# Linear attention, routed experts and SoLU block on one Trainium2 core: TensorE's order in the attention stage written out by hand, with the column-tiled matmuls of a step in one series

## The chip, the cores and the metric

The kernel runs on one core of one Trainium2 chip. The metric is the device time of one execution in microseconds (us), from the median of several runs; less is better.

## The reference

Three blocks follow each other. The change touches the first alone. In it q, k and v have 8 batches, 8 heads, 576 tokens and 64 columns; `w_phi` is 64 x 128.

```python
def phi(x):
    proj = np.einsum('bhsd,df->bhsf', x, w_phi)
    proj = proj - np.max(np.abs(proj), axis=-1, keepdims=True)
    return np.concatenate([np.exp(proj), np.exp(-proj)], axis=-1)
q_p, k_p = (phi(q), phi(k))
kv = np.einsum('bhsf,bhsd->bhfd', k_p, v)
z = np.sum(k_p, axis=2)
num = np.einsum('bhsf,bhfd->bhsd', q_p, kv)
den = np.einsum('bhsf,bhf->bhs', q_p, z)[..., None] + 1e-06
return num / den
```

The second block sends each of the 4608 tokens to one of 8 experts, by the argmax of `x @ w_gate + modality_bias`; the third computes a softmax-weighted hidden layer with a normalization over 4608 x 1024 values.

## The kernel before, in words

**Units and steps.** The attention stage works on units of two batches and four heads: 8 units, numbered by `p2` (a pair of batches) and `g` (which four heads, 0 or 1). A unit is 9 steps (72 in all), one for each 128-row group `i` of tokens: `i` from 0 to 3 belong to the first batch ("half 0"), 5 to 8 to the second ("half 1"), and `i` = 4 holds the last 64 tokens of both. A step has one job of k and one of q (in the last unit, the last four steps take two jobs of k or two of q).

**What a step issues on TensorE.** `s0` (line 239) transposes the k and q rows of the coming step, four 128 x 128 transposes at line 248; ScalarE rounds them to `hi` (line 251) and VectorE takes the rest as `lo` (line 252). `proj` (line 255) multiplies by `w_phi` in three parts, six matmuls of 128 x 256 (lines 260 to 262); VectorE finds the largest absolute value (line 264) and subtracts it (line 266); for k, ScalarE takes the two exponentials into `e` (lines 270, 271). Two steps later (`LAGF`), `accum_kv` (line 274, matmul in line 276) adds v times `e` to the tile `kv`, and `q_features` (line 320) transposes the q values (line 323) and takes their exponentials into `qp`. GpSimd sums `e` into `es` (lines 291, 315).

**Whole and tiled array.** The transposes, the projections and the `kf` matmuls (line 352) use all 128 columns of the array. `kv` uses it in two column tiles of 64 (the profile writes 128\*64, and 64\*64 for `i` = 4, whose halves have 64 rows), `num` (line 397) in two tiles of 64, `den` (line 407) and the sum `z` (line 340) in four tiles of 32.

**After a half.** `finish_kv` (line 336) is a Python generator appended to `tasks` when the last `kv` of a half is in: the sum `z`; `kf`, which turns `kv` round; the transpose of `z` (line 367); four `num` parts and two `den` parts; `finish` (line 444), which transposes `den` (line 462) and `num` (line 477) and divides on VectorE (lines 466 to 479); and, for `g` = 1, `gating` (line 486), a chain of small VectorE instructions from line 492 to line 506, two small matmuls that rank the tokens (lines 514, 515: "the ranking matmuls" below), and more VectorE work up to the scatters to DRAM on GpSimd's queue (line 545). There are nine such chains: one for each half of four pairs of batches, the last of which is cut in two.

**What sets the order.** The loop (from line 607) calls `s0` of the coming step first, then the two projections, then `accum_kv` and `q_features` of two steps before, and resumes the generators `RT` = (0, 1, 2, 1, 0) times at five places. This order is only a priority: in this stage the planner places the instructions of TensorE, VectorE, ScalarE and GpSimd by its own estimate of when each is ready. The order that it finds is fixed in the program; on the chip each engine takes its instructions in that order.

**Buffers.** PSUM has three buffers `tp` (transposes, `kf`), four `mm` (projections, `z`, `num`, `den`) and one `kv`.

Of the kernel before, what the change touches and what calls it, by code (L numbers as in the profile page):

```python
# [8 lines left out]
F32 = mybir.dt.float32  # L9
# [8 lines left out]
P = 128  # L18
# [17 lines left out]
YCOLS = PAD + NTOK  # L36
LAG = 8
LAGF = 2
RT = (0, 1, 2, 1, 0)
BGN = 1  # L40
BGP = 100
PRE = 1
# [146 lines left out]
def attention(ctx, tc, c, cnt, xe, q, k, v, ld, early, m, late):  # L189
# [19 lines left out]
    def load_unit(p2, g):  # L209
        u = Unit()  # L210
        u.p2, u.g = p2, g
        u.src = {}
        for half in range(2):
            b = 2 * p2 + half
            for nm in "kqv":
                u.src[nm, half] = ld.tile([P, 4, 4 * D], F32, name="ld" + nm)
            first = p2 == g == half == 0
            w = 4 * D // (2 if first else 1)
            for c0 in range(0, 4 * D, w):
                for nm, t in (("k", k), ("q", q), ("v", v)):  # L220
# [12 lines left out]
        u.qp = [w2p.tile([P, 2, 4, S], F32, name="qp") for _ in range(2)]  # L233
        u.kv = [None, None]
        u.es = [None, None]
        u.qdone = set()
        return u

# [35 lines left out]
    def accum_kv(u, i, e):  # L274
# [39 lines left out]
            for r in range(2):  # L314
                G.tensor_tensor(out=eo, in0=eo, in1=ev[:, :, r, :], op=ALU.add)  # L315
        if i in (4, 8):
            u.kt = w2p.tile([P, 2, 2 * F], F32, name="kt")
            A.copy(u.kt, u.kv[i // 5])

    def q_features(u, i, x):  # L320
        tp = tps.tile([P, 4, P], F32, name="tp")
# [11 lines left out]
                    tp.rearrange("p (h r) t -> p h (r t)", r=2), AF.Exp, scale=sc,  # L333
                )

    def finish_kv(u, half):
        kt = u.kt
        zp = mmp.tile([P, 2 * F], F32, name="mm")
        for h in range(4):
            T.matmul(  # L340
# [5 lines left out]
        yield  # L346
        kf = w2p.tile([P, 2, 4, D], F32, name="kf")
        gdt = gd[(2 * u.g + half) % 2]
        for j in range(2):
            tp = tps.tile([P, 2, P + 2 * E], F32, name="tp")  # L350
            for fh in range(2):
                T.matmul(
                    tp[:, fh, :], lhsT=kt[:, j, fh * F : (fh + 1) * F], rhs=c.idwg[:, 2 * u.g + j, :],
                    start=(fh == 0), stop=True, skip_group_check=True,
                )
            A.copy(
                kf[:, :, 2 * j : 2 * j + 2, :],
                tp[:, :, 0:P].rearrange("p a (h d) -> p a h d", h=2),
            )
            A.copy(  # L360
                gdt[:, :, 2 * j : 2 * j + 2, 0:E],
                tp[:, :, P : P + 2 * E].rearrange("p a (h e) -> p a h e", h=2),
            )
        yield
        tp = tps.tile([P, 2, P], F32, name="tp")
        for fh in range(2):
            T.transpose(tp[:, fh, :], zs[:, fh, :], c.ident)
        A.copy(gdt[:, :, :, E : E + 1], tp.rearrange("p a (h n) -> p a h n", n=32)[:, :, :, 0:1])
        yield
        tiles = (0, 1, 2, 3) if half == 0 else (5, 6, 7, 8)  # L370
# [6 lines left out]
        def keep(dst, pp, c0, c1):  # L377
            off = half * D
            if half == 0 and c1 == S:
                A.copy(dst(2)[:, 0:D], pp[:, c1 - c0 - D :])  # L380
                c1 -= D
            if half == 1 and c0 == 0:
                A.copy(dst(2)[:, D:P], pp[:, 0:D])
                pp, c0 = pp[:, D:], D
            A.copy(dst(half)[:, c0 - off : c1 - off], pp[:, 0 : c1 - c0])

        last = half == 1 and u is last_unit()
        chunks = (((0, 256), (0, 1)), ((256, S), (2, 3, 4)), ((0, 320), (4, 5, 6)), ((320, S), (7, 8)))
        for ci, ((c0, c1), need) in enumerate(chunks[2 * half : 2 * half + 2]):
            while not u.qdone.issuperset(need):  # L390
                yield
            n = c1 - c0
            for j in range(2):
                pp = mmp.tile([P, n], F32, name="mm")
                for fh in range(2):
                    for hh in range(2):
                        T.matmul(
                            pp[hh * D : (hh + 1) * D, :], lhsT=kf[:, fh, 2 * j + hh, :],
                            rhs=u.qp[half][:, fh, 2 * j + hh, c0:c1],
                            start=(fh == 0), stop=(fh == 1), skip_group_check=True,  # L400
                        )
                keep(lambda x: u.num[x][:, j], pp, c0, c1)
                yield
            pp = mmp.tile([P, n], F32, name="mm")
            for fh in range(2):
                for h in range(4):
                    T.matmul(
                        pp[32 * h : 32 * h + 32, :], lhsT=gdt[:, fh, h, :],
                        rhs=u.qp[half][:, fh, h, c0:c1], tile_position=(0, 32 * h),
                        start=(fh == 0), stop=(fh == 1), skip_group_check=True,  # L410
                    )
            keep(lambda x: u.den[x], pp, c0, c1)
            yield
            if last:
                if ci == 0:
                    yield from finish(u, 2, 0, 1)
                else:
                    yield from pend
                yield from finish(u, 1, 2 * ci, 2)
                if ci == 0:  # L420
                    pend = gating(u, 4, 3)
                    next(pend)
                else:
                    pend = gating(u, 7, 2)
                    for n in range(2):
                        for _ in range(FSTEP):
                            next(pend, None)
                        first_slot(n)
                    yield from pend
        if last:  # L430
            return
        yield from finish(u, half, 0, 4)
        if half == 1:
            yield from finish(u, 2, 0, 1)
        if u.g == 1:
            yield
            yield from gating(u, 4 * half, 4 + half)
            if u.p2 == 2 and half == 1:
                early.pick(cnt[0])
                early.ready = True  # L440

    xt, xs, gs = {}, {}, {}

# [116 lines left out]
            U[ui] = load_unit(*units[ui])  # L560
        return U.get(ui)

    tasks = []

    def first_slot(n):
        if n == 0:
            tp = tps.tile([P, 4, P], F32, name="tp")
# [17 lines left out]
    def last_unit():  # L585
        return U.get(len(units) - 1)

    def run_tasks(n):
        for _ in range(n):
            if not tasks:  # L590
                return
            if next(tasks[0], tasks) is tasks:
                tasks.pop(0)

    unit(0)
    zero = w1p.tile([P, ROW], F32, name="zero")
    G.memset(zero, 0.0)
# [6 lines left out]
    n = len(steps)  # L604
    feats = {}
    late()
    for st in range(n + LAGF):
        if st == 9 * 7 + PRE:
            assert early.ready
            m.prefetch()  # L610
        if st == 9 * 7 + STEP0:
            for i in range(RING0):
                m.split_raw(1, i)
        if st + 1 < n:
# [5 lines left out]
        if st < n:  # L620
            h_ = hl.pop(st)
            feats[st] = []
            for a, (kind, i) in enumerate(steps[st][1]):
                feats[st].append((kind, i, proj(h_, a, kind)))
                run_tasks(RT[1 + a])
        if st >= LAGF:
            u = unit(steps[st - LAGF][0])
            for a, (kind, i, x) in enumerate(feats.pop(st - LAGF)):
                if kind == "k":
                    accum_kv(u, i, x)  # L630
                    if i in (4, 8):
                        tasks.append(finish_kv(u, i // 5))
# [800 lines left out]
```

## Time and profile before

| | us |
|---|---|
| median of 3 runs (lowest to highest) | 1386.82 (1385.80 to 1387.13) |
| span of the profiled execution, first to last instruction | 1384.0 |
| attention on TensorE in that span | 7 to 459 |

The profiled execution is told by its span; the runs are times of the device, a little more than a span. The profile is of one execution. A group of rows gives a line of the kernel, engine, operation, output and inputs, and how often; a time on the left of a timeline row is the start in the span, the next the busy time. Matmuls are pipelined: one is shown busy for longer than the distance to the next start, so what the array gives to one is read from start to start. An idle time stands with what ended it.

### The profile page before, as it was taken

How to read it: one execution, taken by the hardware profiler on the slowest of the kernel's cores; microseconds unless marked ns; L12 is line 12 of the kernel's file. 1: busy time of each engine (PE TensorE's matmuls, PEld its weight loads, DVE VectorE, ACT ScalarE, POOL GpSimd, SP SyncE). 2: the span in 40 equal slices, each digit the busy share in tenths (PEclk: the TensorE clock that was granted, in tenths of full speed). 3: DMA queues.
4: the chain of work that ended last, by engine and by line, in shares of the span. 5: the costliest groups of instructions: out<-in, count | busy, mean ns of one | idle time of the engine just before them, and what ended most of it. 6: DMA issues, size and time to landing. Idle time of an engine off the chain costs nothing.

```text
span 1384.0 us, 25538 instructions
## 1 busy us (share of the span) xinstructions
PE 1338.4 (97%) x9522; PEld 1100.7 (80%) x9522; DVE 829.0 (60%) x1524; ACT 660.0 (48%) x1254; POOL 530.5 (38%) x540
## 2 busy tenths in 40 slices
PE   8999999999999989899899999999999999999997
PEld 6666676666666789899899999998989877778885
DVE  7666866767766748889997544443444333334443
ACT  5564665556555425354456444444444333334332
POOL 6555655654664413343323222323323222223331
PEclk9999999999999999999999999999999999999998
DMA  8622232222131223232532111111234154502110
GB/s 230 191 58 91 97 89 85 89 71 79 47 108 62 86 56 93 77 92 62 185 98 70 47 46 54 32 54 46 76 116 157 42 172 156 160 32 61 39 39 23
DMA packets 123120, 120.09 MB, mean 87 GB/s; under 512 B 35664, under 2 KB 109552, under 8 KB 122992
## 3 DMA queue, kind: packets, MB, share of 16 engines
q1 hardware_dynamic: 117008, 99.30, 23.9%
q0 software_dynamic: 5824, 19.04, 3.8%
q8 instruction: 77, 1.26, 0.4%
q14 instruction: 51, 0.42, 0.1%
q10 hardware_dynamic: 160, 0.07, 0.0%
HBM read 148.32 MB, written 33.02 MB: 131 GB/s over the span
## 4 chain that ended last, share of the span: by engine, by line
PE 51%; DVE 7%; issue 4%; ACT 1%; POOL 0%; POOLq 0%; ACTq 0%; DVEq 0%
PE tp L974 32%; PE h L974 15%; PE tp L998 2%; DVE wlo L832 2%; DVE wab L906 2%; PE tp L804 1%; ACT whi L831 1%; PE tp L1249 1%; PE tp L1233 1%; DVE wab L914 0%; DVE w L832 0%; DVE hTl L989 0%; ACT hTh L988 0%; DVE xTl L794 0%; DVE wab L903 0%
## 5 line engine op out<-in xcount | busy, mean ns | idle before, releaser
L315 POOL TENSOR_TENSOR es<-es,e 128x512 f32<-128x512 f32 x128 | 164.1, 1288 | 132.3 <-ACT e L271 120.6
L264 DVE TENSOR_REDUCE m<-mm 128x4 f32<-128x512 f32 x144 | 97.6, 682 | 64.0 <-PE mm L262 62.7
L974 PE MATMUL tp<-hTh,wlo 128*128 128x256 f32 x432 | 123.3, 285 | 8.7 <-DVE wlo L832 8.7
L974 PE MATMUL tp<-hTl,whi 128*128 128x256 f32 x432 | 123.4, 286 | 4.9 <-DVE hTl L989 4.9
L974 PE MATMUL tp<-xTh,whi 128*128 128x256 f32 x432 | 122.5, 283 | 2.2 <-PEq L1312 2.2
L974 PE MATMUL tp<-hTh,whi 128*128 128x256 f32 x432 | 122.6, 284 | 0.0
L974 PE MATMUL tp<-xTh,wlo 128*128 128x256 f32 x432 | 121.6, 282 | 1.0 <-DVE wlo L832 0.7
L974 PE MATMUL tp<-xTl,whi 128*128 128x256 f32 x432 | 121.2, 281 | 0.0
L1133 DVE TENSOR_REDUCE s_mx<-h 128x1 f32<-128x512 f32 x72 | 46.4, 686 | 118.2 <-PE h L974 118.2
L1169 POOL DMA_INDIRECT out_dram<-wab,gt x36 | 38.3, 1063 | 201.9 <-ACT wab L1168 200.8
L1138 ACT ACTIVATE ex<-h,s_mx,gt 128x1024 f32<-128x1024 f32 x36 | 43.4, 1206 | 119.7 <-DVE s_mx L1135 65.9
L260 PE MATMUL mm<-wphi_hi,hi 128*128 128x256 f32 x288 | 90.7, 318 | 3.5 <-ACT hi L251 1.9
L974 PEld LDWEIGHTS tp<-hTh,wlo 128*128 128x128 f32 x432 | 83.3, 193 | 9.8 <-DVE wlo L832 9.5
L974 PEld LDWEIGHTS tp<-hTl,whi 128*128 128x128 f32 x432 | 83.4, 193 | 6.3 <-DVE hTl L989 6.1
L974 PEld LDWEIGHTS tp<-xTh,whi 128*128 128x128 f32 x432 | 82.1, 190 | 2.8 <-ACTq L1312 2.4
L832 POOL TENSOR_TENSOR yTl<-yin,yTh 128x512 fp32r<-128x512 f32 x36 | 46.4, 1290 | 97.7 <-ACT yTh L831 97.6
L974 PEld LDWEIGHTS tp<-hTh,whi 128*128 128x128 f32 x432 | 83.4, 193 | 0.5
L974 PEld LDWEIGHTS tp<-xTh,wlo 128*128 128x128 f32 x432 | 81.9, 190 | 1.4 <-DVE wlo L832 0.9
L262 PE MATMUL mm<-wphi_hi,lo 128*128 128x256 f32 x288 | 82.6, 294 | 0.3 <-DVE lo L252 0.3
L974 PEld LDWEIGHTS tp<-xTl,whi 128*128 128x128 f32 x432 | 82.0, 190 | 0.4
L276 PE MATMUL kv<-e,ldv 128*64 128x256 f32 x512 | 80.6, 394 | 0.9 <-ACT e L271 0.9
L261 PE MATMUL mm<-wphi_lo,hi 128*128 128x256 f32 x288 | 80.5, 282 | 0.0
(427 smaller groups left out, 3951.9 us busy)
## 6 DMA issues: line engine op xcount, KB each, us to landing
ldk<-in_moe_w_dram SPq DMA_DIRECT2D x66, 512.0 KB
ldv<-in_moe_w_dram SPq DMA_DIRECT2D x66, 512.0 KB
ldq<-in_moe_w_dram SPq DMA_DIRECT2D x44, 512.0 KB
yd<-yo SPq DMA_DIRECT2D x36, 256.0 KB
yin<-yd SPq DMA_DIRECT2D x18, 512.0 KB
xin<-xe SPq DMA_DIRECT2D x16, 512.0 KB
ldk<-in_k_dram SPq DMA_DIRECT2D x15, 512.0 KB
ldq<-in_q_dram SPq DMA_DIRECT2D x15, 512.0 KB
```

The lines of the kernel that those rows point to most:

```text
L260: T.matmul(o, lhsT=hi[:, 2 * a + j, :], rhs=c.wphi_hi, start=(j == 0), stop=False, skip_group_check=True)
L261: T.matmul(o, lhsT=hi[:, 2 * a + j, :], rhs=c.wphi_lo, start=False, stop=False, skip_group_check=True)
L262: T.matmul(o, lhsT=lo[:, 2 * a + j, :], rhs=c.wphi_hi, start=False, stop=True, skip_group_check=True)
L264: V.tensor_reduce(out=m, in_=pj, axis=AX.X, op=ALU.max, apply_absolute_value=True)
L276: T.matmul(u.kv[half][(h % 2) * D : (h % 2 + 1) * D, h // 2, :], lhsT=lhsT, rhs=rhs, start=first, stop=last, skip_group_check=True,)
L315: G.tensor_tensor(out=eo, in0=eo, in1=ev[:, :, r, :], op=ALU.add)
L832: eng.tensor_tensor(out=lo, in0=src, in1=hi.bitcast(F32), op=ALU.subtract)
L906: V.tensor_scalar(out=a, in0=b, scalar1=-0x800000, scalar2=None, op0=ALU.bitwise_and)
L974: T.matmul(o, lhsT=l, rhs=r, start=first and n == 0, stop=last and n == 2, skip_group_check=True)
L1133: V.tensor_reduce(out=mx, in_=h[:, sl], axis=AX.X, op=ALU.max, negate=True)
L1138: A.activation(ex, h, AF.Exp, bias=mx, scale=g, accum_out=sm)
L1169: ins = G.indirect_dma_start(out=out, out_offset=bass.IndirectOffsetOnAxis(ap=ys.pop(i)[2].bitcast(I32), axis=0), in_=ob, in_offset=None,)
```

## The change

From here on TensorE takes its instructions in the attention stage in the order in which the program calls them; the other engines are still placed by the planner. The generator of a half becomes a list of items of four kinds: "f" for work on the whole array (`kf`, the transpose of `z`, then `finish` and `gating` as a chain), "64" for a `num` part, "32" for `z` or a `den` part, "0" for the choice of output tiles. A step is now: transposes of q features, projection of k, one "f", projection of q, one "f", `s0` of the coming step, one "f", then `kv`, up to two "64" and up to one "32". The last half runs as a generator of its own, `finish_last`, once all else is done. Function bodies that only move are left out below.

```diff
-RT = (0, 1, 2, 1, 0)
+FSLOT = (1, 1, 1)
+COLS64 = 2
+COLS32 = 1
+TAIL = 1
...
+    ctx.enter_context(tc.manual_schedule(engines={mybir.EngineType.PE}))
...
+    class Item:
+        def __init__(self, kind, fn, after=(), ready=None):
+            self.kind, self.fn, self.after, self.ready, self.done = kind, fn, after, ready, False
+            items.append(self)
+
+        def runnable(self):
+            return all(x.done for x in self.after) and (self.ready is None or self.ready())
...
+    def run_items(kind, count):
+        ran = 0
+        while ran < count:
+            it = next((x for x in items if x.kind == kind and x.runnable()), None)
+            if it is None:
+                break
...
+    def finish_kv(u, half):
+        at = step[0]
+        zi = Item("32", lambda: z_sum(u, half), ready=lambda: step[0] > at)
+        kfs = [Item("f", lambda j=j: kf_part(u, half, j)) for j in range(2)]
+        zt = Item("f", lambda: z_part(u, half), after=[zi])
+        begin = Item("0", lambda: outputs(u, half))
+        parts = []
+        for ci, (_, need) in enumerate(CHUNKS[half]):
+            ok = lambda need=need: u.qdone.issuperset(need)
+            for j in range(2):
+                parts.append(Item("64", lambda ci=ci, j=j: num_part(u, half, ci, j), after=[begin, kfs[j]], ready=ok))
+            parts.append(Item("32", lambda ci=ci: den_part(u, half, ci), after=[begin, zt, *kfs], ready=ok))
+
+        def rest():
+            yield from finish(u, half, 0, 4)
+            if half == 1:
+                yield from finish(u, 2, 0, 1)
+            if u.g == 1:
                 yield
+                yield from gating(u, 4 * half, 4 + half)
+                if u.p2 == 2 and half == 1:
+                    early.pick(cnt[0])
+                    early.ready = True
+
+        Chain("f", rest(), after=parts)
...
     for st in range(n + LAGF):
+        step[0] = st
...
+        run_items("0", 2)
...
+        q_next()
+        if st < n:
+            h_ = hl.pop(st)
+            feats[st] = []
+            for a, (kind, i) in enumerate(steps[st][1]):
+                feats[st].append((kind, i, proj(h_, a, kind)))
+                run_items("f", FSLOT[a])
+                if a == 0:
+                    q_next()
+        else:
+            q_next()
         if st + 1 < n:
             ui, jobs = steps[st + 1]
             if ("k", 5) in jobs:
                 unit(ui + 1)
             hl[st + 1] = s0(unit(ui), jobs)
-        run_tasks(RT[0])
...
+        run_items("f", FSLOT[2])
+        for i, x in kjobs:
+            accum_kv(u_old, i, x)
+            if i in (4, 8):
+                if i == 8 and u_old is last_unit():
+                    tail.append(finish_last(u_old))
                 else:
-                    q_features(u, i, x)
-                    u.qdone.add(i)
-                run_tasks(RT[3 + a])
-    while tasks:
-        run_tasks(1)
+                    finish_kv(u_old, i // 5)
+        run_items("0", 2)
+        run_items("64", COLS64)
+        run_items("32", COLS32)
+        if st >= n and tail:
+            for _ in range(TAIL):
+                next(tail[0], None)
+    while items:
+        for kind in ("0", "f", "64", "32"):
+            run_items(kind, 1)
+        step[0] += 1
+    for _ in tail[0]:
+        pass
```

## Rows read from the trace of the kernel before

**Rows 1.** The page: busy time of the engines, share of the span, instructions
```profile
PE 1338.4 (97%) x9522; PEld 1100.7 (80%) x9522; DVE 829.0 (60%) x1524; ACT 660.0 (48%) x1254; POOL 530.5 (38%) x540
```

**Rows 2.** Windows: stretch and its length, busy us by engine, clock, DMA share, GB/s
```profile
227.16:339.55 112.39, 111.14 (x907) 75.17 (x907) 78.17 (x158) 65.79 (x163) 63.47 (x58) 1.00 0.26 85
```

**Rows 3.** Waits of TensorE, 20 to 440 us: total us, times, longest
```profile
PE mm L260 <- DVE g_sm L522: 1.6, 3, 0.5
PE kv L276 <- ACT e L271: 0.9, 3, 0.3
PE tp L352 <- ACT qp L331: 0.5, 3, 0.2
PE mm L514 <- DVE g_oh L506: 0.5, 3, 0.2
PE mm L262 <- DVE lo L252: 0.3, 1, 0.3
```

**Rows 4.** Timeline of TensorE, 312 to 319 us: kv in pieces, then whole
```profile
312.74 0.65 PE L276 MATMUL kv<-e,ldv 128*64 128x256 f32 x4
313.32 0.66 PE L323 MATMUL tp<-ident,xsq 128*128 128x128 f32 x4
313.91 0.65 PE L276 MATMUL kv<-e,ldv 128*64 128x256 f32 x4
...
317.67 1.08 PE L276 MATMUL kv<-e,ldv 128*64 128x256 f32 x8
318.58 1.03 PE L397 MATMUL mm<-qp,kf 128*64 128x256 f32 x8
```

**Rows 5.** Timeline of TensorE, 303 to 324 us: transposes alone, kv of two forms, den
```profile
303.17 0.60 PE L477 MATMUL tp<-ident,num 128*128 128x128 f32 x4
303.60 0.38 PE L462 MATMUL tp<-ident,den 128*128 128x128 f32 x2
...
305.09 1.08 PE L276 MATMUL kv<-e,ldv 128*64 128x256 f32 x8
306.11 1.08 PE L276 MATMUL kv<-e,ldrv 64*64 64x256 f32 x8
...
322.11 0.28 PE L261 MATMUL mm<-wphi_lo,hi 128*128 128x256 f32 x1
322.22 0.28 PE L262 MATMUL mm<-wphi_hi,lo 128*128 128x256 f32 x1
322.43 1.07 PE L407 MATMUL mm<-qp,gd 128*32 128x256 f32 x16
323.43 0.38 PE L260 MATMUL mm<-wphi_hi,hi 128*128 128x256 f32 x1
323.65 0.28 PE L261 MATMUL mm<-wphi_lo,hi 128*128 128x256 f32 x1
```

**Rows 6.** Timeline of TensorE: first and last of 166 series of column-tiled matmuls
```profile
17.70 1.08 PE L276 MATMUL kv<-e,ldv 128*64 128x256 f32 x8
...
457.01 0.63 PE L407 MATMUL mm<-qp,gd 128*32 128x256 f32 x4
```

**Rows 7.** Timeline of TensorE: den transposes and ranking matmuls, half 0, half 1
```profile
107.96 0.44 PE L462 MATMUL tp<-ident,den 128*128 128x128 f32 x2
...
117.22 0.18 PE L514 MATMUL mm<-g_oh,tri_bf 128*128 128x32 bf16 x1 [0.16 <-DVE g_oh L506]
...
139.97 0.27 PE L462 MATMUL tp<-ident,den 128*128 128x128 f32 x1
...
146.40 0.18 PE L514 MATMUL mm<-g_oh,tri_bf 128*128 128x40 bf16 x1
```

**Rows 8.** Groups of VectorE by form, 227.16 to 339.55 us, the costliest: total and mean ns
```profile
L264 DVE TENSOR_REDUCE m<-mm 128x4 f32<-128x512 f32 x36 | 24.4, 682 | 15.7 <-PE mm L262 15.3
```

**Rows 9.** Windows behind the attention stage, columns as in rows 2
```profile
495.00:500.00 5.00, 1.58 (x13) 1.41 (x12) 0.00 (x0) 0.97 (x2) 0.00 (x0) 0.95 0.38 105
500.00:505.00 5.00, 5.00 (x33) 5.00 (x32) 4.78 (x5) 3.94 (x7) 0.00 (x0) 0.70 0.01 2
```

More of the change, by code (lines that the diff above doesn't have):

```diff
@@ L235, in load_unit @@
         u.es = [None, None]
+        u.kt, u.zs, u.kf = [None, None], [None, None], [None, None]
         u.qdone = set()
@@ L316, in accum_kv @@
         if i in (4, 8):
-            u.kt = w2p.tile([P, 2, 2 * F], F32, name="kt")
-            A.copy(u.kt, u.kv[i // 5])
+            u.kt[i // 5] = w2p.tile([P, 2, 2 * F], F32, name="kt")
+            A.copy(u.kt[i // 5], u.kv[i // 5])
     def q_features(u, i, x):
@@ L334, in q_features, with __init__, z_sum @@
                 )
-    def finish_kv(u, half):
-        kt = u.kt
+    items = []
+    class Item:
[4 more added lines that the diff above has]
+            return all(x.done for x in self.after) and (self.ready is None or self.ready())
+    class Chain(Item):
+        def __init__(self, kind, gen, after=(), ready=None):
+            super().__init__(kind, None, after, ready)
+            self.gen = gen
+    def run_items(kind, count):
[4 more added lines that the diff above has]
+                break
+            if isinstance(it, Chain):
+                if next(it.gen, items) is not items:
+                    ran += 1
+                    continue
+            else:
+                it.fn()
+            it.done = True
+            items.remove(it)
+            ran += 1
+        return ran
+    step = [0]
+    def z_sum(u, half):
         zp = mmp.tile([P, 2 * F], F32, name="mm")
@@ L345, in finish_kv @@
         A.copy(zs, zp.rearrange("p (a f) -> p a f", a=2))
-        yield
-        kf = w2p.tile([P, 2, 4, D], F32, name="kf")
-        gdt = gd[(2 * u.g + half) % 2]
[L349 to L358, printed above, removed]
-            )
[L360 to L363, printed above, removed]
@@ L364, in finish_kv, with kf_part @@
-        yield
+        u.zs[half] = zs
+    def kf_part(u, half, j):
+        if j == 0:
+            u.kf[half] = w2p.tile([P, 2, 4, D], F32, name="kf")
+        kf = u.kf[half]
+        gdt = gd[(2 * u.g + half) % 2]
+        tp = tps.tile([P, 2, P + 2 * E], F32, name="tp")
+        for fh in range(2):
+            T.matmul(
+                tp[:, fh, :], lhsT=u.kt[half][:, j, fh * F : (fh + 1) * F], rhs=c.idwg[:, 2 * u.g + j, :],
+                start=(fh == 0), stop=True, skip_group_check=True,
+            )
+        A.copy(
+            kf[:, :, 2 * j : 2 * j + 2, :],
+            tp[:, :, 0:P].rearrange("p a (h d) -> p a h d", h=2),
+        )
+        A.copy(
+            gdt[:, :, 2 * j : 2 * j + 2, 0:E],
+            tp[:, :, P : P + 2 * E].rearrange("p a (h e) -> p a h e", h=2),
+        )
@@ L365, in finish_kv, with z_part, keep @@
+    def z_part(u, half):
+        gdt = gd[(2 * u.g + half) % 2]
         tp = tps.tile([P, 2, P], F32, name="tp")
         for fh in range(2):
-            T.transpose(tp[:, fh, :], zs[:, fh, :], c.ident)
+            T.transpose(tp[:, fh, :], u.zs[half][:, fh, :], c.ident)
         A.copy(gdt[:, :, :, E : E + 1], tp.rearrange("p a (h n) -> p a h n", n=32)[:, :, :, 0:1])
-        yield
-        tiles = (0, 1, 2, 3) if half == 0 else (5, 6, 7, 8)
+    def keep(half, dst, pp, c0, c1):
+        off = half * D
+        if half == 0 and c1 == S:
+            A.copy(dst(2)[:, 0:D], pp[:, c1 - c0 - D :])
+            c1 -= D
+        if half == 1 and c0 == 0:
+            A.copy(dst(2)[:, D:P], pp[:, 0:D])
+            pp, c0 = pp[:, D:], D
+        A.copy(dst(half)[:, c0 - off : c1 - off], pp[:, 0 : c1 - c0])
@@ new lines, in attention, with num_part @@
+    CHUNKS = (
+        (((0, 256), (0, 1)), ((256, S), (2, 3, 4))),
+        (((0, 320), (4, 5, 6)), ((320, S), (7, 8))),
+    )
+    def num_part(u, half, ci, j):
+        c0, c1 = CHUNKS[half][ci][0]
+        n = c1 - c0
+        pp = mmp.tile([P, n], F32, name="mm")
+        for fh in range(2):
+            for hh in range(2):
+                T.matmul(
+                    pp[hh * D : (hh + 1) * D, :], lhsT=u.kf[half][:, fh, 2 * j + hh, :],
+                    rhs=u.qp[half][:, fh, 2 * j + hh, c0:c1],
+                    start=(fh == 0), stop=(fh == 1), skip_group_check=True,
+                )
+        keep(half, lambda x: u.num[x][:, j], pp, c0, c1)
@@ new lines, in den_part @@
+    def den_part(u, half, ci):
+        c0, c1 = CHUNKS[half][ci][0]
+        n = c1 - c0
+        gdt = gd[(2 * u.g + half) % 2]
+        pp = mmp.tile([P, n], F32, name="mm")
+        for fh in range(2):
+            for h in range(4):
+                T.matmul(
+                    pp[32 * h : 32 * h + 32, :], lhsT=gdt[:, fh, h, :],
+                    rhs=u.qp[half][:, fh, h, c0:c1], tile_position=(0, 32 * h),
+                    start=(fh == 0), stop=(fh == 1), skip_group_check=True,
+                )
+        keep(half, lambda x: u.den[x], pp, c0, c1)
@@ L371, in finish_kv, with outputs @@
+    def outputs(u, half):
         u.num[half] = w1p.tile([P, 2, 4 * P], F32, name=f"num{half}")
@@ L375, in finish_kv @@
             u.den[2] = w1p.tile([P, P], F32, name="den2")
[L377 to L387, printed above, removed]
@@ L388, in finish_kv @@
-        chunks = (((0, 256), (0, 1)), ((256, S), (2, 3, 4)), ((0, 320), (4, 5, 6)), ((320, S), (7, 8)))
-        for ci, ((c0, c1), need) in enumerate(chunks[2 * half : 2 * half + 2]):
-            while not u.qdone.issuperset(need):
-                yield
-            n = c1 - c0
-            for j in range(2):
[L394 to L402, printed above, removed]
-                yield
[L404 to L412, printed above, removed]
-            yield
[L414 to L440, printed above, removed]
+    def finish_kv(u, half):
[15 more added lines that the diff above has]
+            if u.g == 1:
+                yield
+                yield from gating(u, 4 * half, 4 + half)
[3 more added lines that the diff above has]
+        Chain("f", rest(), after=parts)
@@ new lines, in finish_last @@
+    def finish_last(u):
+        z_sum(u, 1)
+        yield
+        for j in range(2):
+            kf_part(u, 1, j)
+        yield
+        z_part(u, 1)
+        yield
+        outputs(u, 1)
+        for ci in range(2):
+            for j in range(2):
+                num_part(u, 1, ci, j)
+                yield
+            den_part(u, 1, ci)
+            yield
+            if ci == 0:
+                yield from finish(u, 2, 0, 1)
+            else:
+                yield from pend
+            yield from finish(u, 1, 2 * ci, 2)
+            if ci == 0:
+                pend = gating(u, 4, 3)
+                next(pend)
+            else:
+                pend = gating(u, 7, 2)
+                for n in range(2):
+                    for _ in range(FSTEP):
+                        next(pend, None)
+                    first_slot(n)
+                yield from pend
@@ L561, in unit @@
         return U.get(ui)
-    tasks = []
     def first_slot(n):
@@ L586, in last_unit @@
         return U.get(len(units) - 1)
[L588 to L593, printed above, removed]
     unit(0)
@@ L606, in attention @@
     late()
+    tail = []
     for st in range(n + LAGF):
+        step[0] = st
         if st == 9 * 7 + PRE:
@@ L613, in attention, with q_next @@
                 m.split_raw(1, i)
+        run_items("0", 2)
+        old = feats.pop(st - LAGF, ())
+        u_old = unit(steps[st - LAGF][0]) if st >= LAGF else None
+        kjobs = [(i, x) for kind, i, x in old if kind == "k"]
+        qjobs = [(i, x) for kind, i, x in old if kind == "q"]
+        def q_next():
+            if qjobs:
+                i, x = qjobs.pop(0)
+                q_features(u_old, i, x)
+                u_old.qdone.add(i)
+        q_next()
[7 more added lines that the diff above has]
+                    q_next()
+        else:
+            q_next()
         if st + 1 < n:
```

13 lines of the change are left out of this document (removed).

## The prediction, made before the changed kernel had run

> **What bounds the kernel now.** I read the busy line of the page first: TensorE is busy 97% of a span of 1384.0 us [rows 1]. The runs' median is 1386.82, so 2.8 us lie around the span; I make the sum against the span and add them again. Then the window of one pair of units in the middle of the attention stage (the pair before it, from 114.80 us, reads the same to 0.3 us): 112.4 us, TensorE busy 111.1, VectorE 78, ScalarE 66, GpSimd 64, at a granted clock of 1.00, which is 2.4 GHz [rows 2]. The waits of TensorE say the same: between 20 and 440 us only five kinds are listed, 3.8 us together, the largest with 1.6 us in 3 waits [rows 3]. So in this stage TensorE sets the time, and what is worth reading is what its busy time holds. Busy time alone can't tell that; the distances of starts can.
>
> **What a switch costs.** Four transposes among full-array work take 0.43 us from start to start (303.17 to 303.60) [rows 5]. Eight `kv` matmuls followed by more work of two 64-column tiles take 0.91 us, so four take 0.455 [rows 4]. Where they alternate, four `kv` and four transposes take 1.17 us (312.74 to 313.91) [rows 4], which is 1.17 - 0.455 - 0.43 = 0.29 us more. That is one way into column tiles and one way out. Beside projections it is a little dearer: plain ones are 0.11 us apart, the first `den` matmul comes 0.21 behind the last of them, and the first projection after it takes 0.22 to the next [rows 5]. These two distances are 0.21 over the plain ones, and they don't hold what the last `den` matmul loses on the way out. I take 0.31 for a series, whatever its neighbours. A change from one column form to another inside a series: eight `kv` of 128\*64 before a 64\*64 form take 1.02 us (305.09 to 306.11) [rows 5] where 0.91 stands for no change [rows 4], so 0.11, and some more for the slower first pair behind it; I take 0.13.
>
> The Trainium skill, in TensorEngine Tiling (Array Packing), section Tiling Modes, states that changing the tiling mode, and not just the tile, drains the engine. It speaks against a part of this change, since a series that mixes widths drains inside as well. By it an inner change would cost half a series, 0.15, and the sum would be 0.6 us smaller in gain; the trace's 0.11 and more is near that.
>
> **The change part by part.**
>
> Fewer series. Before, 166 series of column-tiled matmuls stand in the stage, from 17.70 to 457.01 us [rows 6], with 24 inner changes. After, I count by walking the new loop: every step that has a `kv` holds one series (70 steps, since four steps of the last unit hold two jobs of k or none), one step behind them has `num` and `den` alone, and the last half makes two: 73. Inner changes: 47 from 64 or 64\*64 to 32 (each `z` and `den` behind a `kv` or `num`), 8 from the 64-row form where `i` = 5 closes what `i` = 4 began; 55. So 93 series fewer, 93 x 0.31 = 28.8 us, and 31 inner changes more, 31 x 0.13 = 4.0 us. Net -24.8 us, all of it on the engine that sets the time. The matmuls themselves keep count, size and clock.
>
> The fixed order, gating. The planner could put other work ahead of a matmul that was not ready; now nothing passes it. The dearest such place is the ranking matmul at line 514, which waits for a chain of VectorE. Before, from the first `den` transpose of the half to this matmul it took 9.26 us in half 0 (107.96 to 117.22) and 6.43 in half 1 (139.97 to 146.40) [rows 7]. After, the loop puts this work between them on TensorE in half 0: seven groups of four transposes (one `den`, two `num`, two `s0`, two `q_features`), 7 x 0.43; four projections of six matmuls at 0.117, 4 x 0.70; two series of `kv`, 2 x (0.91 + 0.31); and `z`, eight matmuls in four tiles, 0.42 and an inner change, 0.55. Sum 8.8 us. In half 1 it is about 6.5 us by the same prices. That would leave a wait of 0.5 us or none. But VectorE does more in the meantime. An instruction on 128 x 512 values takes it 0.68 us [rows 8], and a step has five (line 252 once, 264 and 266 twice). In half 0 the new order puts two steps' worth ahead of the ranking, where one was done before: 5 x 0.68 = 3.4 us later, a wait of up to 3.9 us. In half 1 it is three more, 2.1 us. The lower end is none, for VectorE is still placed by the planner and idles 15.3 us in a pair behind line 262 alone [rows 8]; a gain beyond the few tenths that these waits cost now is excluded. The mean of the upper ends is 3.0 us; nothing speaks for either end, and I take 1.5 us, for eight gatings 12 us, less 2 us of such waits that go [rows 3]. Behind the ranking matmul stand the next projections, so the wait is TensorE's loss, whole.
>
> The fixed order, the rest. `s0` moves from the front of a step to behind its projections, and `hi` and `lo` of the next step must be ready after only `kv` and `q_features`: 0.91 + 0.31 + 0.43 = 1.65 us in a step without `num`, of which ScalarE and VectorE need about 0.6 + 0.68. Where `finish` is in the same step, VectorE has its 0.68 us divisions too, and one of them may come first. Bound: 0 to 0.8 us for each of 16 halves, 0 to 13 us. I take 0.25 each, 4 us: nearer to none, since `num` and `den` cover most steps, and a wait for `lo` was met once between 20 and 440 us [rows 3]. If that cover were gone in all steps, the upper end would hold. With `s0` moves the call that loads a unit, on SP's queue; no load is among TensorE's waits there [rows 3], it is asked four steps ahead, and it costs nothing unless that lead is lost. The scatters follow the ranking on GpSimd's queue, in front of later sums into `es`; GpSimd is busy 64 of 112 us [rows 2], which hides them. The single `num` and `den` tiles, the copies of ScalarE and all other counts stay.
>
> The tail: the last half runs alone at the end, with its chains in the open, as before; I put it into the terms above.
>
> Sum: -24.8 + 12 - 2 + 4 = -10.8 us, 1373.2 for the span, **1376.0 us** for the median. What follows the stage is not touched, and starts earlier by as much.
>
> **The rivals.**
>
> Almost no waits. If VectorE's chain fits into its idle time, the whole saving stays: 1386.8 - 24.8 = 1362 us, and 1358 if the 3.8 us of waits go as well. For it: 34 us of idle VectorE in a pair (112.4 - 78.2) [rows 2], and 9.26 and 6.43 us against 8.8 and 6.5. Against: the idle time lies in steps that are full of `num`, not where `finish` and `gating` are. Chance 0.27.
>
> Slower: the ranking waits take all. At line 514 each wait comes to its upper end, 4 x 3.9 + 4 x 2.1 = 24 us; and TensorE, having stood still, goes on at a lower clock. Behind a stretch in which it was busy 1.58 of 5 us, the next 5 us had a granted clock of 0.70, a mixture of 1.2 and 2.4 GHz with 60% at the lower, 3 us of half speed, 1.5 us lost [rows 9]. Four times that is 6 us. Sum -24.8 + 24 - 2 + 4 + 6 = +7.2, 1394 us. It decides from a mean wait of 2.9 us in eight gatings, (24.8 + 2 - 4) / 8. Against it: the clock was 1.00 throughout the pair [rows 2]. Chance 0.18. The Trainium skill, in TensorE: Matmul & The Clock Gate, section Part 2, says that matmuls stay in program order and only weight loads are pulled ahead. By that rule nothing softens these waits; the waits of rows 3 are of this kind. In its section on oscillation of the clock it warns of the loss after idle gaps; that the trace shows behind the stage, and in the attention stage not.
>
> No difference. The stage is shorter, but what follows waits for something that does not move with it: TensorE is busy only 1.58 of the 5 us before 500 already [rows 9], and such a wait could grow by what was saved. Or the waits add up to 23 to 27 us by many small ones. 1384 to 1389 us. Against: the loads and tables there follow from the stage's own chains. Chance 0.13.
>
> **How the numbers follow.** The forecast, about half of the saving kept (1367 to 1383), has 0.42. The likeliest is 1376. No change within 0.2%, 2.8 us, can be told by measurement. Faster: forecast and first rival, 0.69; same 0.13; slower 0.18. The range goes from the first rival's lower end, 1358, to the slower rival's 1394; outside is what lies beyond both, about 0.15 to 0.2.
>
> **What would show it.** Right: about 73 series in the stage, starts inside them 0.21 us apart, and a pair of units in 105 to 110 us; waits at line 514 between 1 and 2.5 us. First rival: a pair in 105 us or less, with waits of TensorE as few as now. Slower rival: waits over 3 us at line 514 and a granted clock under 1.00 behind them. The prediction is wrong if the switch price, 0.31, does not go away with the series, or if new waits stand at places that I did not name, above all at the projections (lines 260, 262) or for `tp` buffers.

## The result, and the profile of the changed kernel

The changed kernel takes 1396.62 us (median of 4 runs, 1396.06 to 1399.91) against 1386.78 of the kernel before beside it: a ratio of 1.0076, 95% interval 1.0062 to 1.0090. It is slower, by 9.8 us, and lies outside the range that was given. Its profiled execution has a span of 1394.7 us.

The page's busy line of the changed kernel answers to [rows 1]: the same 9522 matmuls, and TensorE is busy 17.6 us less in a span that is 10.7 us longer.

```profile
PE 1320.8 (95%) x9522; PEld 1105.4 (79%) x9522; DVE 820.5 (59%) x1524; ACT 666.2 (48%) x1254; POOL 529.5 (38%) x540
```

The series were joined as foretold. Counted in the trace there are 73 with 55 inner changes. What took the gain is in the waits of TensorE from 20 to 440 us, the view of [rows 3] (total us, times, longest):

```profile
PE mm L591 <- DVE g_oh L583: 9.3, 3, 3.1
PE tp L554 <- DVE gs L545: 8.7, 14, 1.1
PE mm L267 <- DVE lo L257: 6.5, 6, 4.9
PE mm L434 <- ACT kf L397: 1.6, 3, 0.5
PE mm L448 <- DVE xsk L271: 0.6, 1, 0.6
```

Line 591 is the ranking matmul (514 before), 267 the third projection (262), 554 the transposes of `num` (477). All five kinds of before came to 3.8 us; here the first three come to 24.5. The next view is of windows, columns as in [rows 2]; the last row is a pair of units, as the row there; the first three are stretches of 5 us around its end.

```profile
268.00:273.00 5.00, 2.02 (x18) 1.85 (x17) 4.65 (x14) 3.00 (x7) 2.32 (x4) 0.90 0.39 121
273.00:278.00 5.00, 4.88 (x23) 3.70 (x23) 3.44 (x12) 1.31 (x3) 2.69 (x4) 0.50 0.00 0
278.00:283.00 5.00, 5.00 (x42) 3.75 (x40) 2.87 (x6) 2.71 (x8) 2.94 (x3) 0.92 0.30 111
163.41:275.95 112.54, 106.08 (x909) 76.42 (x907) 76.04 (x159) 67.17 (x162) 64.47 (x59) 0.97 0.27 85
```

A pair takes 112.5 us, as before, but TensorE is busy 5.1 us less in it, and its clock is 0.97: the saving was made in busy time, and handed out again as waits and as half clock.

**The ranking wait.** The timeline of TensorE shows it in half 1 (start, busy time, and the idle time before with what ended it in brackets); the first row is half 0, where there is none.

```profile
239.35 0.19 PE L591 MATMUL mm<-g_oh,tri_bf 128*128 128x32 bf16 x1
...
265.96 1.08 PE L281 MATMUL kv<-e,ldv 128*64 128x256 f32 x8
266.98 0.64 PE L378 MATMUL mm<-es,ones 128*32 128x256 f32 x8
...
269.64 0.38 PE L253 MATMUL tp<-ident,ldq 128*128 128x128 f32 x2
273.12 0.19 PE L591 MATMUL mm<-g_oh,tri_bf 128*128 128x40 bf16 x1 [3.09 <-DVE g_oh L583]
273.14 0.20 PE L592 MATMUL mm<-g_oh,ones_bf 128*128 128x40 bf16 x1
273.27 1.98 PE L281 MATMUL kv<-e,ldv 128*64 128x256 f32 x8
275.18 1.12 PE L328 MATMUL tp<-ident,xsq 128*128 128x128 f32 x4
```

`kv`'s eight take 1.02 us from start to start at 265.96 and 1.91 at 273.27, behind the wait: this is the granted clock of 0.50 in the window from 273, the lower of the two levels, 1.2 GHz. From 273.27 to 278.66 stand eight `kv`, four transposes and twelve projections, 5.39 us; at the full clock the same take 1.02 + 0.41 + 1.46 (read at 265.96, 267.55 and 267.96) = 2.89. So the wait of 3.1 us costs another 2.5 behind it. It comes three times (161.5, 273.1 and 385.7 us); behind the last the loss is 2.5 again (385.87 to 391.25), behind the first 1.6 (161.67 to 166.12), for there `kv` still ran at the full clock.

On VectorE the end of the chain to `g_oh` stands behind four instructions on 128 x 512 values from 270.32 on, 0.6 us apart:

```profile
270.32 0.68 DVE L269 TENSOR_REDUCE m<-mm 128x4 f32<-128x512 f32 x1
270.92 0.68 DVE L271 TENSOR_TENSOR xsk<-mm,m 128x512 f32<-128x512 f32 x1
271.51 0.18 DVE L581 TENSOR_REDUCE g_mx<-g_first 128x5 f32<-128x40 f32 x1
271.62 0.15 DVE L600 TENSOR_SCALAR g_sm<-g_sm 128x5 f32<-128x5 f32 x1
271.68 0.68 DVE L271 TENSOR_TENSOR xsq<-mm,m 128x512 f32<-128x512 f32 x1
272.28 0.68 DVE L257 TENSOR_TENSOR lo<-tp,hi 128x512 fp32r<-128x512 f32 x1
272.88 0.18 DVE L583 TENSOR_TENSOR g_oh<-rev,g_mx 128x40 bf16<-128x40 f32 x1
```

**The start.** Measured from the first projection of step 0, that of step 7 comes after 24.50 us before and after 36.97 now. Three timelines show why: TensorE, ScalarE and VectorE of the changed kernel.

```profile
15.37 0.38 PE L253 MATMUL tp<-ident,ldq 128*128 128x128 f32 x2
15.59 0.60 PE L328 MATMUL tp<-ident,xsq 128*128 128x128 f32 x4
17.77 0.38 PE L265 MATMUL mm<-wphi_hi,hi 128*128 128x256 f32 x1 [1.58 <-ACT hi L256]
...
34.98 0.28 PE L266 MATMUL mm<-wphi_lo,hi 128*128 128x256 f32 x1
40.12 0.58 PE L267 MATMUL mm<-wphi_hi,lo 128*128 128x256 f32 x1 [4.86 <-DVE lo L257]
```

```profile
16.09 0.63 ACT L275 ACTIVATE e<-xsk 128x512 f32<-128x512 f32 x1 [3.00 <-DVE xsk L271]
16.63 0.61 ACT L276 ACTIVATE e<-xsk 128x512 f32<-128x512 f32 x1
17.15 0.57 ACT L256 CAST hi<-tp 128x512 fp32r<-128x512 f32 x1
```

```profile
33.34 0.76 DVE L178 CAST modf<-mod 128x36 f32<-128x36 int32 x1 [1.84 <-DMA mod<-in_moe_modality_id_dram]
34.13 2.43 DVE L183 TENSOR_SCALAR msk<-modf 128x36 f32<-128x36 f32 x2
36.48 0.45 DVE L184 TENSOR_TENSOR bias<-msk,mb 128x288 f32<-128x288 f32 x1
...
39.38 0.68 DVE L257 TENSOR_TENSOR lo<-tp,hi 128x512 fp32r<-128x512 f32 x1
```

The transposes of `s0` are issued by 15.59 us, at the end of their step; `hi` then stands behind the two exponentials of the step before on ScalarE, and TensorE has four transposes to do meanwhile. Later `lo` stands behind VectorE's work on the modality bias, which `late()` calls ahead of the loop, and which waited for its load: 4.86 us for all of TensorE.

**The balance** at the last `den` of the stage: the waits in it, without the first loads, are 34 us against 7 before, 27 more; half clock costs 1.6 + 2.5 + 2.5 behind the ranking, and some 3 us at the start by the distances from 19.4 to 22.9 and from 40.1 to 43.4 us. 27 + 6.6 + 3 - 24.8 = +12 us; the traces show +11.0 (467.36 - 7.84 against 457.26 - 8.72).

### The profile page after: what moved, and what is told of

Read it like the earlier page. It is cut to its first block, busy times and chain, and to the rows that moved or that the text cites. A ratio compares the mean times of both kernels' runs of the same rounds, so it can differ in the third digit from the quotient of the medians.

```text
span 1394.7 us, 25444 instructions
## 1 busy us (share of the span) xinstructions
PE 1320.8 (95%) x9522; PEld 1105.4 (79%) x9522; DVE 820.5 (59%) x1524; ACT 666.2 (48%) x1254; POOL 529.5 (38%) x540
## 4 chain that ended last, share of the span: by engine, by line
PE 49%; DVE 7%; issue 4%; ACT 2%; DMA 0%; SPq 0%; POOL 0%; POOLq 0%; ACTq 0%; DVEq 0%
PE tp L1067 30%; PE h L1067 14%; PE tp L1091 2%; DVE wlo L925 2%; DVE wab L999 2%; ACT whi L924 1%; DVE w L925 1%; PE tp L897 1%; PE tp L1342 1%; PE tp L1326 1%; DVE wab L1007 1%; DMA ldk<-in_moe_w_dram 0%; DVE wab L996 0%; DVE xTl L887 0%; ACT hTh L1081 0%
## 5 line engine op out<-in xcount | busy, mean ns | idle before, releaser
L267 PE MATMUL mm<-wphi_hi,lo 128*128 128x256 f32 x288 | 85.4, 297 | 7.0 <-DVE lo L257 7.0
L887 DVE TENSOR_TENSOR lnTl<-tp,lnTh 128x512 fp32r<-128x512 f32 x74 | 47.6, 685 | 53.6 <-ACT lnTh L886 53.6
```

The costliest lines, as they stand in the source:

```text
L267: T.matmul(o, lhsT=lo[:, 2 * a + j, :], rhs=c.wphi_hi, start=False, stop=True, skip_group_check=True)
L887: self.tc.nc.vector.tensor_tensor(out=lo, in0=tp, in1=hi.bitcast(F32), op=ALU.subtract)
```

## The experiments

All times stand beside runs of the kernel before on the same chip. To compare across chips I take the difference of the two medians; for the change itself it is +9.8 us.

| kernel | median us | ratio to before, interval | difference us |
|---|---|---|---|
| e1_fixed_only | 1413.40 | 1.0192 (1.0175 to 1.0209) | +27.2 |
| e2_series_free | 1397.63 | 1.0082 (1.0065 to 1.0099) | +11.4 |
| e8_broken | 1406.37 | 1.0143 (1.0126 to 1.0160) | +20.1 |
| e3_late | 1390.99 | 1.0038 (1.0026 to 1.0049) | +4.8 |
| e4_rank2 | 1400.64 | 1.0093 (1.0074 to 1.0113) | +14.4 |
| e5_tp4 | 1394.06 | 1.0053 (1.0036 to 1.0070) | +7.8 |
| e9_late_tp4 | 1388.00 | 1.0008 (0.9999 to 1.0018) | +1.7 |
| e7_late_rank | 1394.91 | 1.0077 (1.0056 to 1.0099) | +9.1 |
| e6_all | 1383.38 | 0.9979 (0.9967 to 0.9990) | -2.9 |
| e11_s0_mid | 1383.93 | 0.9989 (0.9980 to 0.9999) | -1.9 |
| e10_all_s0mid | 1372.51 | 0.9908 (0.9892 to 0.9925) | -13.3 |
| e12_rank3half0 | 1361.63 | 0.9831 (0.9815 to 0.9848) | -23.6 |

**The two halves of the change, alone.** e1_fixed_only is the kernel before with TensorE's order fixed as the program calls it:

```diff
+    ctx.enter_context(tc.manual_schedule(engines={mybir.EngineType.PE}))
```

> The kernel before with one line added: TensorE takes its instructions in program order; steps, generators and their places stay. Theory (the series save about 25 us, and the waits of a fixed order eat more than that): without the saving and with a program order that has about as many series as there are pieces of column-tiled work, it is slower than the changed kernel: 1400 to 1450 us. Rival (series save nothing, the fixed order alone costs the 10 us): about as long as the changed kernel, 1393 to 1400 us.

The time is in the theory's range, but its reason was only half right: the saving is not missing. Counted in the trace there are 94 series with 46 inner changes, so the fixed order alone joins most of them (72 x 0.31 - 22 x 0.13 = 19.5 us by the prices of the prediction), and the waits take more than that. The largest, from the waits of TensorE:

```profile
PE mm L515 <- DVE g_oh L507: 31.6, 6, 5.7
```

In the old call order the ranking matmuls wait 4.9 us in each half 0 and 5.7 in each half 1. The planner had been hiding this; in the new order it is 10.8 us in four. e2_series_free is the change without that line.

> The changed kernel without the line that fixes TensorE's order: the items and the new step remain as a priority for the planner. Theory: the planner fills waits again, but splits series again, to between 100 and 160 of them; TensorE's waits in the stage fall back to under 10 us; 1375 to 1390 us. Rival (the step order itself costs, not its being fixed): 1393 us or more.

Missed, and in the rival's range: +11.4 us. The planner cuts the series again (157, with 38 inner changes) and the listed waits are short (the largest kind 5.8 us in 7), yet a pair of units takes 117.2 and 115.6 us. So the new call order used as a mere priority is not better than the old one. In part these are waits after all, 4.5 and 3.7 us in the two pairs, in many short ones, against 1.2 in a pair before; where they and the rest come from I did not settle.

**Does the price of a series hold?** e8_broken does the same work, with the q transposes of a step between `kv` and `num`, `z`, `den`:

```diff
-        q_next()
         if st < n:
...
-                if a == 0:
-                    q_next()
-        else:
-            q_next()
...
         for i, x in kjobs:
             accum_kv(u_old, i, x)
...
+        q_next()
+        q_next()
```

> The changed kernel with the four transposes of the q features moved from the front of the next step to between kv and num or den of the step before, so that the same work in nearly the same order cuts the series of each step with num, den or z in two: about 45 to 50 series more, 20 inner changes fewer. What stands between s0 and the next projection stays the same work. Theory (a series costs 0.31 us on TensorE's path): 47 x 0.31 - 20 x 0.13 = 12 us more, 1405 to 1412 us. Rival (TensorE waits for the others anyway, so the switches hide in its waits): under 4 us more, 1394 to 1401 us.

121 series and 35 inner changes: 48 x 0.31 - 20 x 0.13 = 12.3 us by the prices of the prediction; measured 20.1 - 9.8 = 10.3, while the waits for `tp` tiles fell from 8.7 to 5.5 us. The price holds, within what those waits give back. What the prediction took from the Trainium skill (TensorEngine Tiling (Array Packing), section Tiling Modes) can be read again here: `kv` in front of a 32-column form takes 1.02 us (265.96 to 266.98), 0.11 over the 0.91 of [rows 4], as at the change of [rows 5].

**One cause at a time.** e3_late takes the bias work off the start:

```diff
-    late()
     tail = []
     for st in range(n + LAGF):
         step[0] = st
+        if st == 12:
+            late()
```

> The changed kernel, with the call that loads modality_id and works out the gating bias moved from ahead of the loop into step 12. Theory: the wait of 4.9 us for lo at 40 us, in which VectorE stands before the modality load and then works on the bias, goes, and the stretch of half clock behind it: 5 to 7 us less, 1390 to 1392 us. Rival (the first steps are bound by the chain transpose, hi, lo, projection anyway): 1395 to 1397 us.

As the theory said: the longest wait for `lo` falls from 4.9 to 0.4 us, and 5.0 us go. e4_rank2 issues the ranking matmuls of half 1 two turns later:

```diff
+        if n == 5:
+            yield
+            yield
         rkp = mmp.tile([P, 2, n, E], F32, name="mm")
```

> The changed kernel, with the ranking matmuls of the five-tile gatings (half 1 of the first three pairs) two places of kind f later. Theory: the three waits of 3.3 us at the ranking matmul go, and the 2 us that half clock costs behind each: 13 to 16 us less, 1381 to 1384 us. Rival (VectorE is the limit there, and the wait comes back at lo or at a tp buffer): 1393 to 1397 us.

A miss, 4.6 us slower than the change. The ranking wait is gone but for 1.5 us in the tail, and in its place the waits of TensorE list:

```profile
PE mm L267 <- DVE lo L257: 11.2, 14, 4.9
PE tp L554 <- DVE gs L545: 8.7, 14, 1.1
PE tp L253 <- ACT gd L401: 7.0, 3, 3.0
```

The third is new. The five scatters behind the ranking, now later, stand in GpSimd's queue ahead of a sum into `es` (GpSimd's timeline), and a copy of `kf` on ScalarE, which must free a `tp` tile, starts while that sum runs. That the sum holds the copy is not shown: what ended its idle time the trace calls only "remote".

```profile
287.44 1.02 POOL L625 DMA_INDIRECT xe<-xt,g_dsti  x1 [2.57 <-DVE g_dsti L623]
...
292.56 0.96 POOL L625 DMA_INDIRECT xe<-xt,g_dsti  x1 [0.30 <-issue]
293.54 1.27 POOL L320 TENSOR_TENSOR es<-es,e 128x512 f32<-128x512 f32 x1
```

```profile
294.53 0.37 ACT L397 COPY kf<-tp 128x256 f32<-128x256 f32 x1 [3.24 <-remote]
```

e5_tp4 gives the transposes a fourth tile, at the cost of one of the projections':

```diff
-    tps = ctx.enter_context(tc.tile_pool(name="a_tp", bufs=3, space=PSUM))
-    mmp = ctx.enter_context(tc.tile_pool(name="a_mm", bufs=4, space=PSUM))
+    tps = ctx.enter_context(tc.tile_pool(name="a_tp", bufs=4, space=PSUM))
+    mmp = ctx.enter_context(tc.tile_pool(name="a_mm", bufs=3, space=PSUM))
```

> The changed kernel with four tp buffers and three mm buffers instead of three and four. Theory: the 14 waits at the num transposes, which end with the division step that frees a tp buffer (8.7 us together), go: 6 to 9 us less, 1388 to 1391 us. Rival (three mm buffers, of which a full step wants five, bring waits of the same size at projections and num): 1394 to 1402 us.

At the lower end of the rival's range: 2.0 us less than the change, and since the two intervals overlap, a gain is not shown. The 8.7 us at line 554 are gone, but at most some of them are saved, for the projections are reached sooner and wait for `lo` instead (7.0 us in 8 waits before this edit):

```profile
PE mm L267 <- DVE lo L257: 13.6, 16, 4.9
PE mm L591 <- DVE g_oh L583: 11.4, 5, 3.1
```

e9_late_tp4 joins e3_late and e5_tp4, e7_late_rank joins e3_late and e4_rank2, and e6_all has all three.

> Both the late bias and the four tp buffers. Theory: the two gains lie in different stretches and add: 1382 to 1386 us. Rival (the mm buffers take the second back): 1389 to 1396 us.

> The change with late() in step 12 and the ranking of half 1 two turns later, but three tp buffers as before. Theory (the later ranking pays only with a fourth tp buffer, since with three the copies of ScalarE that follow it hold TensorE up): the gain of late(), 5.6 us, and the loss of e4_rank2, 4.0 us, add up to 1393 to 1397 us. Rival (what spoiled e4_rank2 was its start, not the tp buffers): 1385 us or less.

> Late bias, four tp buffers, and the ranking matmuls two places later. Theory (with a fourth tp buffer the wait that had come back at s0 goes): 1372 to 1380 us, faster than the kernel before. Rival (GpSimd's scatters or ScalarE hold the next kf, whatever the buffers): the same as without the later ranking, 1382 to 1390 us.

e9 missed its theory's range and came out just under its rival's, 3.1 us better than e3_late. With three `tp` tiles the later ranking costs 4.3 us (e3 to e7, as the theory there had it); with four it gives 4.6 (e9 to e6). So the wait of the ranking could be removed for gain only together with the wait for a `tp` tile that came in its place. e6_all missed its range; 13.3 us in 22 waits for `lo` were left in it. That pointed to the place of `s0`.

**The place of s0.** e11_s0_mid is the change with the transposes of the coming step between the two projections, nothing else:

```diff
                 if a == 0:
                     q_next()
+                    if st + 1 < n:
+                        ui, jobs = steps[st + 1]
+                        if ("k", 5) in jobs:
+                            unit(ui + 1)
+                        hl[st + 1] = s0(unit(ui), jobs)
...
-        if st + 1 < n:
-            ui, jobs = steps[st + 1]
-            if ("k", 5) in jobs:
-                unit(ui + 1)
-            hl[st + 1] = s0(unit(ui), jobs)
```

> Theory (the transposes s0 of the next step now stand behind both projections, so hi and lo come late; that is the term 'the fixed order, the rest'): with s0 between the two projections TensorE has six more matmuls (0.7 us) to do before it needs hi and lo. Waits of line 265 on hi (4.1 us) and the small ones of line 267 on lo (2.1 of 7.0) fall to about 1 us together; the one of 4.9 us at 40 us stays, since VectorE has its bias work in front of lo there. Waits for tp tiles stay. 1391 to 1394 us. Rival (the three tp buffers set the pace, and a tp tile taken earlier is one that num's transposes or kf lack): waits of line 554 or line 393 grow by what hi and lo lose, 1395 us or more.

It gives 11.7 us, far more than either expected, and ends a little below the kernel before. The waits of TensorE, 0 to 475 us, for `lo` and `hi` in the change, then those of e11:

```profile
PE mm L267 <- DVE lo L257: 7.0, 8, 4.9
PE mm L265 <- ACT hi L256: 4.1, 3, 1.6
```

```profile
PE mm L591 <- DVE g_oh L583: 15.5, 7, 2.5
PE tp L554 <- DVE lo L257: 4.0, 13, 0.3
...
PE mm L267 <- DVE lo L257: 2.6, 1, 2.6
PE mm L265 <- ACT hi L256: 1.3, 1, 1.3
```

`hi` and `lo` together fall from 11.1 to 3.9 us, and line 554's tiles from 8.7 to 4.6 (0.6 of it with another releaser), while the ranking, reached sooner, waits more (15.5 against 10.8). From step 0, step 9 comes after 51.75 us in the change and 44.27 here, step 71 after 432.88 and 421.81: two thirds of it is won in the first nine steps, where little but `kv` and the q transposes stands between `s0` and the projections.

**All together.** e10_all_s0mid is e6_all with `s0` there; e12_rank3half0 also issues the ranking of half 0 one turn later, and with it that of the two pieces of the last half.

> Kernel of e6_all with s0 between the two projections. Theory (what is left of waits in e6_all is lo, 13.3 us in 22, and hi, 3.6 in 3, because s0 stands too late): they fall to 4 us or less together, 1372 to 1376 us. Rival (VectorE itself is late there, since finish and gating stand in front of lo in its order, so an earlier s0 only changes which wait is met): 1380 us or more, with waits of line 267 on lo over 9 us still.

> Kernel of e10_all_s0mid with the ranking of half 0 one turn later too (there three waits of 2.9 us stand at 120, 227 and 333 us, and the granted clock is 0.97 in the pair of units behind 276 us). Theory (a place still sets the wait, and now nothing else is near): the three waits and the half clock behind them go, 8 to 12 us, 1361 to 1365 us. Rival (as in e4_rank2: the later half 0 meets the front of half 1, and the wait comes back at kf, num or tp): 1370 us or more, with new waits of lines 434, 448 or 554 of over 6 us together.

Both times are as their theory said: 10.4 us for the place of `s0` and 10.3 for the later ranking of half 0. But its three waits did not go: they are 2.7 us each in e10 and still 1.6 in e12, and the waits of the ranking fall from 10.0 to 6.6 us in all. More of the gain lies in the clock: in windows of 50 us from 50 to 400 it is 0.98, 0.97 and 0.93 in three of e10's, some 6 us by the lost share, and 1.00 in all of e12's. e12 is faster than both kernels: 1361.63 us (1360.48 to 1362.56), 23.6 less than before. Two pairs of units in its windows, the view of [rows 2], and its largest wait from 20 to 430 us:

```profile
147.15:251.77 104.62, 102.34 (x909) 74.83 (x908) 74.73 (x158) 68.05 (x163) 63.71 (x58) 1.00 0.29 92
251.77:356.37 104.60, 102.30 (x909) 74.81 (x908) 74.68 (x158) 68.08 (x163) 63.62 (x58) 1.00 0.24 78
```

```profile
PE mm L594 <- DVE g_oh L583: 6.6, 4, 1.8
```

A pair is 7.8 us shorter than before and the clock is back at 1.00. Whether the kernel before would also gain from a later `late()` was not tried, nor was each edit of e12 taken out of it again. VectorE's own order, in which four long instructions stand ahead of `g_oh`, was left to the planner in every run.

## Why the prediction was wrong

**Fewer series: right.** 73 series and 55 inner changes were counted, and e8 bears out the price. So does a pair: it has 44 series and 5 inner changes before and 18 and 14 after, 26 x 0.31 - 9 x 0.13 = 6.9 us by the prices; TensorE is 5.1 us less busy in it, 7.6 without the 2.5 us of half clock that it holds. e12, with the same 73 series, lies 23.6 us under before, where the net saving was put at 24.8. That these are so close is in part luck: its stage holds 13 us of waits, against 7 before, and its pair is 8.8 us less busy, with other edits in it. The prediction's first rival, "almost no waits", 1362 us and a pair of 105 us or less, is about where e12 comes; it is not what the change as made does.

**"The fixed order, the rest": the step that failed most.** It put 0.25 us on each of 16 halves, 4 us, "nearer to none, since `num` and `den` cover most steps". e11 shows 11.7 us for the place of `s0` alone, near the upper end of 13, which the prediction had set aside for the case that the cover is gone. It is gone in the first steps, which the step did not look at: there is no half to finish yet, and VectorE has the bias work. The prediction also read the waits of before from 20 us on, and so took nothing from the start of the stage. And it did not cost the `tp` tiles at all, though it named them as a place that would prove it wrong: 8.7 us in 14 waits. With the 11.1 us for `hi` and `lo` these waits are 19.8 us, against some 2 before, where the term said 4.

**Gating: right size in the wrong half, and without its second price.** The sum was 8 waits of 1.5 us, 12 us. There are four, 10.8 us: three of 3.1 us in half 1, where the upper bound was 2.1, one in the tail, and none in half 0, where it was 3.9. From the first `den` transpose to the ranking TensorE took 10.4 us in half 0 (229.00 to 239.35, put at 8.8), 0.8 of them waits at lines 554 and 267, and VectorE was done after 8.4. In half 1 TensorE was there 6.6 us after the last `den` transpose (263.39), as the 6.5 had it, but VectorE took 9.7, where 6.43 + 2.1 was the bound. That bound counted three more instructions of 0.68 us on VectorE; the trace has four of them in the last 2.6 us of the chain alone. (The starts in [rows 7], 107.96 and 139.97, are those of the last `den` transposes of their halves; the prediction calls them the first, which come at 105.50 and 133.33.) Then the half clock, 1.6 to 2.5 us three times. The prediction had it, at 1.5 us, only in the slower rival, from a mean wait of 2.9 us on; here it came behind each wait of 3.1 us, whatever the mean.

**The rivals.** The slower rival named the direction and the clock, and gave 1394 us; 1396.6 came, but by another sum: its ranking waits were to take 24 us, and took 10.8. The rest was `lo`, `hi` and `tp`.

**The rule on program order.** The prediction cited the Trainium skill, TensorE: Matmul & The Clock Gate, Part 2, that matmuls stay in program order. The trace agrees: from 269.64 to 273.12 us no projection or `kv` passes the waiting ranking. That was weighed at the ranking alone; it holds for the other waits too, as from 34.98 to 40.12 us, where nothing passes line 267.

## What to carry to other kernels

When an order that a planner had softened is fixed by hand, the count of what is saved is the easy half; for every operand of the fixed engine write down which other engine makes it, what stands ahead of it in that engine's queue, and how much work the fixed engine has in between, in the first steps and the last as well as in the steady ones. Waits of an engine whose order is fixed stand behind each other: taking out one (e4_rank2) can cost time until the one that comes in its place is out as well (the fourth `tp` tile, in e6_all), so try such edits together before dropping one. A wait of some 3 us on TensorE should be priced with the stretch at half clock that can follow it.

## What the runs showed of the hardware that was not expected

A stand of 3.1 us inside a stage that is otherwise full could bring the granted clock to 0.50 for the 5 us behind it (at 273.1 us; TensorE was busy 2.02 us of the 5 before), and that cost nearly as much as the wait itself. It does not do so each time, and the length of the wait alone does not tell. In e5_tp4 the wait of 3.1 us at 385.7 leaves the clock at 1.00. In e10_all_s0mid three waits of 2.7 us end at 120.2, 227.2 and 332.7 us, with TensorE 2.3 us busy in the 5 before each, and the 5 us behind them have a granted clock of 0.66, 1.00 and 0.50:

```profile
120.20:125.20 5.00, 4.99 (x30) 4.14 (x31) 4.67 (x10) 1.26 (x4) 3.92 (x4) 0.66 0.23 52
227.20:232.20 5.00, 4.99 (x42) 3.53 (x42) 4.69 (x10) 1.85 (x7) 3.93 (x4) 1.00 0.23 52
332.70:337.70 5.00, 4.98 (x24) 4.05 (x25) 4.64 (x10) 1.26 (x4) 3.93 (x4) 0.50 0.02 3
```

In e12_rank3half0 the ranking waits of half 0 are 1.6 us, and the clock stays at 1.00 in both windows that hold one; behind the wait of 1.8 us in its tail, which ends at 423.2, it falls again:

```profile
425.00:430.00 5.00, 4.67 (x35) 2.08 (x32) 0.52 (x4) 1.46 (x6) 3.10 (x4) 0.75 0.28 107
```
